# Set-up of a fused spectral-filter and MLP kernel: pools freed tile by tile, and the last inverse unit ahead of the first half's outputs

## The chip, the cores and the metric

The kernel runs on one core of one Trainium2 chip. The metric is the device time of one execution in microseconds, lower is better. Before the change it took 786.47 us (median of three runs, 786.09 to 787.12). All runs in this document were in the fast state: no run was more than 1.5% above the fastest of its kernel. Verdicts are given at 2%, with a 95% interval for the ratio of two kernels. The whole effect studied here is under 0.5%, so every verdict reads "same", and what decides is the stretches within the traces.

The engines go by the profile's names: PE (TensorE, the matmuls), ACT (ScalarE), DVE (VectorE), POOL (GpSimd) and SP (SyncE, which issues transfers). A result of PE lands in a bank of PSUM; "to evacuate" it means that ACT or DVE copies it from there to SBUF.

## The reference

```python
# x: 8 x 3008 x 256, filters 1505 x 256, w_in 256 x 2048, w_out 2048 x 256, all float32
X = np.fft.rfft(x, axis=1)
Y = X * (filt_r + 1j * filt_i)[None]
y = np.fft.irfft(Y, n=3008, axis=1)            # 8 x 3008 x 256
t = y.reshape(24064, 256)
h = t @ w_in                                   # 24064 x 2048
g = h * (1.0 / (1.0 + np.exp(-beta * h)))
out = (g @ w_out).astype(np.float32)           # 24064 x 256
```

## The kernel before

The transform of length 3008 = 47 x 64 is done as four stages of small matmuls with tables (`t1`, `t2`, `t3` and its rotated copy `t3s`, `t4`). The first batch goes through SBUF as fast as it can, because nothing else can run until its output `y` is there. That is the set-up, about the first 43 us. After it comes a loop of 47 blocks of 16 steps: two `hps` matmuls, a Silu on ACT into `gT`, four `acc` matmuls, with the transforms of batches 1 to 7 threaded in by a plan (`at(step, function)`).

In the set-up the inverse half is a chain for each half `e` of the 256 columns: three units `s3_0` (16 matmuls each, evacuated to `zT`), four turns `z_turn` (eight PE transposes each, evacuated to `zz0`), then outputs, either eight small ones `f_0` (4 matmuls, 376 columns to evacuate) or four big ones `s4_0` (8 matmuls, 752 columns). Units 0 to 2 are the first half, 3 to 5 the second. The first half uses `f_0`, the second `s4_0`.

```python
tw = dict(reuse_waits="tile")     # a pool on released memory waits tile by tile, not for all users
spsum = right.enter_context(tc.tile_pool(name="spsum", bufs=3, space=bass.MemoryType.PSUM))  # 3 x 2 banks
tpsum = right.enter_context(tc.tile_pool(name="tpsum", bufs=2, space=bass.MemoryType.PSUM))  # 2 x 1 bank
units = [(0, 0), (1, 0), (2, 0), (0, 1), (1, 1), (2, 1)]     # (group of tables, half e)

def evac(dst, src, on_act, scale=None):
    if on_act:
        nc.scalar.activation(dst, src, ACT.Copy, scale=1.0 if scale is None else scale)
    elif scale is None:
        nc.vector.tensor_copy(dst, src)
    else:
        nc.vector.tensor_scalar_mul(dst, src, scale)

def bank2(shape, dt=F32):
    return spsum.tile(shape, dt, name="sps", tag="sps")
def turn8():
    return tpsum.tile([P, KH, P], BF16, name="tps", tag="tps")

def z_turn(e, hh, on_act, wide=False):            # transposes of zT -> zz0
    tp = bank2([P, KH, P], BF16) if wide else turn8()
    ...
def s3_0(n, engines=(True,)):                     # pq_t x tables -> zT
    one = len(engines) == 1
    tiles = [bank2([P, KH, P])]
    tiles.append(tiles[0] if one else bank2([P, KH, P]))   # two engines: two PSUM tiles
    ...
def f_0(e, u, on_act):                            # 4 output groups, a tpsum tile
def s4_0(e, hh, on_act):                          # 8 output groups, an spsum tile
# ...
s3_0(3)
s2_0(5)
f_0(0, 0, True); f_0(0, 1, True)
z_turn(0, 2, True); z_turn(0, 3, True)
s3_0(4)
f_0(0, 2, True); f_0(0, 3, True); f_0(0, 4, False)
s3_0(5, (False, True))
f_0(0, 5, True); f_0(0, 6, False); f_0(0, 7, True)
z_turn(1, 0, False); z_turn(1, 1, True); z_turn(1, 2, False, True); z_turn(1, 3, True, True)
s4_0(1, 0, False); s4_0(1, 1, True); s4_0(1, 2, False); s4_0(1, 3, True)
```

(The order of the tail is put several calls to a line here.) A `True` in a call means that ACT evacuates, `False` that DVE does. The fourth argument of `z_turn` takes a wide PSUM buffer. Which of the three wide or two small buffers a tile gets is decided when the program is built. It isn't a strict rotation, and the source doesn't show it.

Of the kernel before, what the change touches and what calls it, by code (L numbers as in the profile page):

```python
# [36 lines left out]
def kernel(  # L37
# [30 lines left out]
        )  # L68
    )

    dpool = ctx.enter_context(tc.tile_pool(name="dram_scratch", bufs=2, space=bass.MemoryType.DRAM))
    consts = ctx.enter_context(tc.tile_pool(name="consts", bufs=1))
    wpool = ctx.enter_context(tc.tile_pool(name="wpool", bufs=1))

    xpool = ctx.enter_context(tc.tile_pool(name="xpool", bufs=4))
    apool = ctx.enter_context(tc.tile_pool(name="apool", bufs=4))
    ypools = [ctx.enter_context(tc.tile_pool(name="ypool0", bufs=1))]
    fr_sb = consts.tile([P, NK, D], F32, name="fr_sb", tag="fr_sb")
    fi_sb = consts.tile([P, NK, D], F32, name="fi_sb", tag="fi_sb")
# [29 lines left out]
# [7 lines that stand above are left out]
# [3 lines left out]
    def rpool(name, stack=right, **kw):  # L119
        return stack.enter_context(tc.tile_pool(name=name, side="right", **kw))  # L120

    tw = dict(reuse_waits="tile")
    spsum = right.enter_context(
        tc.tile_pool(name="spsum", bufs=3, space=bass.MemoryType.PSUM)
    )
    tpsum = right.enter_context(
        tc.tile_pool(name="tpsum", bufs=2, space=bass.MemoryType.PSUM)
    )
    sp = rpool("setup", bufs=1)

# [5 lines that stand above are left out]
# [216 lines left out]
        nc.sync.dma_start(rows[:, g * JG : (g + 1) * JG, :], st["a1", b][:])  # L352

    left = ExitStack()
    wst = ctx.enter_context(tc.tile_pool(name="wstage", bufs=2))
    zpool0 = left.enter_context(tc.tile_pool(name="zpool0", bufs=1))
    WG = 4
    wstage = {}
# [33 lines left out]
    def z_turn(e, hh, on_act, wide=False):  # L392
        tp = bank2([P, KH, P], BF16) if wide else turn8()
        for i in range(KH):
            j0 = (hh * KH + i) * KP
            nc.tensor.transpose(tp[:, i, :], zT[e][:, j0 : j0 + P], ident[:])  # L396
        evac(zz0[:, hh * KH : (hh + 1) * KH, e * P : (e + 1) * P], tp[:KP], on_act)

    def s4_0(e, hh, on_act):
        ps = bank2([P, JG, P])  # L400
        for i in range(JG):
            nc.tensor.matmul(
                ps[:, i, :NP],
                lhsT=zz0[:, hh * JG + i, e * P : (e + 1) * P],
                rhs=t4[:],
                start=True,
                stop=True,
            )
        dst = ys[0][:, e, :].rearrange("p (n j) -> p n j", j=J)
        evac(  # L410
            dst[:, :, hh * JG : (hh + 1) * JG],
            ps[:, :, :NP].rearrange("p j n -> p n j"),
            on_act,
            inv_scale,
        )

    pq = {}
    r_p0 = ExitStack()
    p0pool = rpool("p0pool", r_p0, bufs=2)

    def s2_0(n):
        kg, e = units[n]
        ds = slice(e * P, (e + 1) * P)
        ks = slice(kg * KH, (kg + 1) * KH)
        ps = bank2([P, KH, P])
        for kk_ in range(KH):
            k1 = kg * KH + kk_
            nc.tensor.matmul(
                ps[:, kk_, :], lhsT=t2[:, k1, :], rhs=a0[:, k1, ds], start=True, stop=True
            )  # L430
        for c, filt in enumerate((fr_sb, fi_sb)):
            r_t = p0pool.tile([P, KH, P], BF16, name="pq_t", tag=f"pq{c}")
            nc.vector.tensor_tensor(r_t[:], ps[:], filt[:, ks, ds], ALU.mult)
            pq[n, c] = r_t

    def s3_0(n, engines=(True,)):
        kg, e = units[n]
        one = len(engines) == 1
        tiles = [bank2([P, KH, P])]
        tiles.append(tiles[0] if one else bank2([P, KH, P]))  # L440
        for c, tab in enumerate((t3, t3s)):
            src = pq.pop((n, c))
            for kk_ in range(KH):
                nc.tensor.matmul(  # L444
                    tiles[kk_ // 4][:, kk_, :],
                    lhsT=src[:, kk_, :],
                    rhs=tab[:, kg * KH + kk_, :],
                    start=c == 0 and kk_ % 4 == 0,
                    stop=c == 1,
                    skip_group_check=True,  # L450
                )
        kq = P // J
        dst = zT[e][:, :WZ].rearrange("p (j k) -> p j k", k=KP)
        for h, on_act in enumerate(engines):
            n0, n1 = (0, KH) if one else (4 * h, 4 * h + 4)
            k0 = kg * KH
            evac(
                dst[:, :, (k0 + n0) * kq : (k0 + n1) * kq],
                tiles[h][:, n0:n1, :].rearrange("p k (c j) -> p j (k c)", j=J),
                on_act,  # L460
            )
# [9 lines left out]
    def f_0(e, u, on_act):  # L471
        ps = tpsum.tile([P, 4, P], F32, name="tps", tag="tps")
        for i in range(4):
            nc.tensor.matmul(
                ps[:, i, :NP],
                lhsT=zz0[:, 4 * u + i, e * P : (e + 1) * P],
                rhs=t4[:],
                start=True,
                stop=True,
            )  # L480
        dst = ys[0][:, e, :].rearrange("p (n j) -> p n j", j=J)
        evac(
            dst[:, :, 4 * u : 4 * u + 4],
            ps[:, :, :NP].rearrange("p j n -> p n j"),
            on_act,
            inv_scale,
        )
# [40 lines left out]
    s3_0(3)  # L528
    s2_0(5)
    f_0(0, 0, True)  # L530
    f_0(0, 1, True)
    z_turn(0, 2, True)
    z_turn(0, 3, True)
    s3_0(4)
    f_0(0, 2, True)
    f_0(0, 3, True)
    f_0(0, 4, False)
    s3_0(5, (False, True))
    f_0(0, 5, True)
    f_0(0, 6, False)  # L540
    f_0(0, 7, True)
    z_turn(1, 0, False)
    z_turn(1, 1, True)
    z_turn(1, 2, False, True)
    z_turn(1, 3, True, True)
    s4_0(1, 0, False)
    s4_0(1, 1, True)
    s4_0(1, 2, False)
    s4_0(1, 3, True)
    r_p0.close()  # L550
    r_sr.close()
    right.close()
# [242 lines left out]
```

## Time and profile before

| quantity, before | value |
|---|---|
| time, median of 3 | 786.47 us |
| span of the profiled run | 785.6 us |
| first `hps` matmul of the loop | 42.71 us |
| PE idle in the loop (waits from 42.7 us on) | 2.3 us in three waits |
| stall of PE on the first scratch load (`a<-d`) | 1.2 us |

The windows view gives busy time by stretch. Its columns are the stretch and its length, then busy us and instructions of PE, PE's weight loads, DVE, ACT and POOL, the granted TensorE clock, the mean busy share of the DMA engines as the tool adds it up (it can pass 1), and GB/s. These lines are of before.

```profile
30.00:40.00 10.00, 6.97 (x124) 6.42 (x121) 5.28 (x7) 7.63 (x13) 5.59 (x6) 1.00 1.06 214
...
50.00:60.00 10.00, 10.00 (x69) 6.65 (x68) 1.37 (x2) 8.21 (x14) 4.78 (x4) 1.00 0.78 216
...
200.00:785.00 585.00, 580.75 (x4487) 412.54 (x4485) 306.84 (x479) 412.67 (x601) 84.42 (x77) 1.00 0.36 100
```

There are two regimes. In the loop PE hardly rests (580.75 of 585 us), so it only moves as a block. In the set-up no engine is full: PE 6.97 and ACT 7.63 of 10 us between 30 and 40 us. There each engine waits for another, and only the chain of dependencies counts. A change of the set-up is worth the time by which it lets the block start earlier.

The timeline of PE in before, from the first turns on (start, duration, engine, source line, operation, tiles, count, and in brackets the idle time before it and what ended it). L444 is `s3_0`, L396 `z_turn`, L474 `f_0`, L726 and L746 the loop.

```profile
26.55 0.62 PE L396 MATMUL tps<-ident,zT 128*128 128x128 bf16 x8 [0.22 <-ACT zT L111]
28.28 0.61 PE L396 MATMUL tps<-ident,zT 128*128 128x128 bf16 x8 [1.11 <-ACT zz L111]
...
33.91 0.33 PE L474 MATMUL tps<-t,zz 96*128 96x94 bf16 x4 [0.51 <-ACT zz L111]
35.19 0.33 PE L474 MATMUL tps<-t,zz 96*128 96x94 bf16 x4 [0.96 <-ACT y L111]
35.36 0.61 PE L444 MATMUL sps<-t,pq_t 128*128 128x128 bf16 x8
...
42.71 0.59 PE L726 MATMUL hps<-y,win_sb 128*128 128x512 bf16 x2 [0.89 <-ACT y L111]
...
45.38 0.60 PE L746 MATMUL acc<-wout_sb,gT 128*128 128x256 bf16 x4
```

The line at 35.36 is what the change aims at: the last inverse unit, `s3_0(5)`, starts behind small outputs that waited 0.51 and 0.96 us for small PSUM buffers. Everything of the second half hangs on that unit. The line at 28.28: two turns in a row were given the same small bank, and the second one waited 1.11 us for the evacuation of the first.

Two clocks are used from here on. **S** is the stretch from the start of the first turn to the start of the first `acc` group: 45.38 - 26.55 = 18.83 us in before. The **body** is from that `acc` group to the end of the span, 785.6 - 45.38 = 740.2 us.

The list of PE's waits in the loop of before (from 42.7 us on; total us, times, longest) has two entries. The first is a load from scratch memory in the loop, at about 62.6 us.

```profile
PE ps L588 <- DMA a<-d: 1.2, 1, 1.2
PE hps L726 <- ACT y L111: 1.1, 2, 0.9
```

### The profile page before, as it was taken

To read this page: it belongs to the slowest core of one execution; us is meant where nothing else is said; L and a number is where in the kernel's file an instruction comes from. 1 tells how busy PE (TensorE), PEld (TensorE's weight loads), DVE (VectorE), ACT (ScalarE), POOL (GpSimd) and SP (SyncE) were. 2 spreads that over 40 slices of the span, in tenths; PEclk is the share of its full clock that TensorE was granted. 3 is DMA by queue.
4 is the path that set the end of the run, shared out by engine and by line. 5 is a ranking of instruction groups with operands and counts; after the bars stand their busy time and mean duration, and the time that the engine had idled before them with its cause. 6 is when DMAs were issued, how large, how long until landed. Compare 5 with 4: busy or idle time off the path is not lost.

```text
span 785.6 us, 15256 instructions
## 1 busy us (share of the span) xinstructions
PE 768.7 (98%) x6071; PEld 544.7 (69%) x6071; DVE 437.1 (56%) x679; ACT 560.8 (71%) x826; POOL 151.9 (19%) x160
## 2 busy tenths in 40 slices
PE   8699999999999999999999999999999999999997
PEld 5666767766677666866678666786667767676664
DVE  7746754777557665566655665466655666321001
ACT  6787867767676766777667776677766777777775
POOL 6723400332012220122201222012200222000000
PEclk9999999999999999999999999999999999999999
DMA  9968286233831349123580426612164111500101
GB/s 175 228 175 196 79 223 169 68 88 96 240 95 51 95 126 256 39 76 107 115 241 29 120 62 156 199 57 86 48 188 121 61 48 49 155 28 28 55 28 55
DMA packets 89819, 88.51 MB, mean 113 GB/s; under 512 B 5692, under 2 KB 80956, under 8 KB 89748
## 3 DMA queue, kind: packets, MB, share of 16 engines
q1 hardware_dynamic: 85716, 73.94, 32.1%
q0 software_dynamic: 4032, 13.60, 10.3%
q8 instruction: 47, 0.77, 0.4%
q14 instruction: 24, 0.20, 0.1%
HBM read 54.47 MB, written 46.66 MB: 129 GB/s over the span
## 4 chain that ended last, share of the span: by engine, by line
PE 94%; ACT 3%; DMA 1%; DVE 1%; issue 0%; POOL 0%; POOLq 0%; DVEq 0%; ACTq 0%
PE acc L746 42%; PE hps L726 41%; PE ps L572 3%; PE ps L639 2%; PE ps L588 2%; PE ps L617 2%; DMA a<-d 1%; ACT zz L111 1%; ACT zT L111 1%; ACT y L111 0%; ACT aT L111 0%; PE tps L396 0%; ACT t3s L291 0%; PE sps L444 0%; ACT a L111 0%
## 5 line engine op out<-in xcount | busy, mean ns | idle before, releaser
L735 ACT ACTIVATE gT<-hps,beta_sb 128x512 bf16<-128x512 f32 x752 | 516.9, 687 | 208.8 <-PE hps L726 206.2
L746 PE MATMUL acc<-wout_sb,gT 128*128 128x256 bf16 x3008 | 453.4, 272 | 0.0
L726 PE MATMUL hps<-y,win_sb 128*128 128x512 bf16 (+7 forms) x1728 | 448.0, 351 | 1.1 <-ACT y L111 1.1
L746 PEld LDWEIGHTS <-gT 128*128 128x128 bf16 x3008 | 287.5, 98 | 126.2 <-issue 1.2
L607 POOL TENSOR_TENSOR yh<-a_t,b_t 128x512 bf16<-128x512 f32 x84 | 106.4, 1267 | 421.8 <-DVE b_t L606 420.9
L726 PEld LDWEIGHTS <-win_sb 128*128 128x128 bf16 x1728 | 164.9, 98 | 25.2 <-issue 1.2
L113 DVE COPY ost<-acc 128x512 f32<-128x512 f32 x93 | 59.9, 686 | 147.6 <-PE acc L746 147.6
L113 DVE CAST a<-ps 96x512 bf16<-96x512 f32 x104 | 70.8, 685 | 52.5 <-PE ps L572 48.4
L602 DVE TENSOR_TENSOR a_t<-ps,fr_sb 128x512 f32<-128x512 f32 x84 | 58.1, 692 | 71.3 <-PE ps L588 70.8
L115 DVE TENSOR_SCALAR y<-ps 128x376 bf16<-128x376 f32 x104 | 56.0, 548 | 59.3 <-PE ps L639 59.1
L603 DVE SCALAR_TENSOR_TENSOR b_t<-ps,fi_sb 64x512 f32<-64x512 f32 x84 | 58.2, 692 | 1.1
L606 DVE TENSOR_TENSOR b_t<-ps,fi_sb 64x512 f32<-64x512 f32 x84 | 57.4, 683 | 1.1
L113 DVE CAST z<-ps 128x512 bf16<-128x512 f32 x72 | 49.3, 684 | 1.7 <-PE ps L617 0.8
L639 PEld LDWEIGHTS <-zz 96*128 96x128 bf16 x448 | 29.8, 98 | 22.9
L572 PE MATMUL ps<-xg,t 94*96 94x512 bf16 x112 | 41.5, 381 | 0.0
L639 PE MATMUL ps<-t,zz 96*128 96x94 bf16 x448 | 34.7, 205 | 0.0
L588 PE MATMUL ps<-a,t 128*128 128x256 bf16 x168 | 32.1, 273 | 1.2 <-DMA a<-d 1.2
L617 PE MATMUL ps<-yh,t 128*128 128x256 bf16 x168 | 32.1, 273 | 0.0
L617 PEld LDWEIGHTS <-t 128*128 128x128 bf16 x168 | 16.2, 98 | 17.7
L588 PEld LDWEIGHTS <-t 128*128 128x128 bf16 x168 | 16.1, 98 | 16.6 <-issue 1.5
L171 POOL DMA_DIRECT2D xg<-in_x_dram x24 | 12.4, 519 | 56.5 <-PE ps L572 56.5
L572 PEld LDWEIGHTS <-t 94*96 94x96 bf16 x112 | 13.8, 123 | 10.5
(104 smaller groups left out, 184.3 us busy)
## 6 DMA issues: line engine op xcount, KB each, us to landing
out_dram<-ost SPq DMA_DIRECT2D x46, 512.0 KB, 3.0
d<-a SPq DMA_DIRECT2D x28, 384.0 KB, 4.5
a<-d SPq DMA_DIRECT2D x28, 384.0 KB, 5.2
d<-z SPq DMA_DIRECT2D x28, 384.0 KB, 3.7
zz<-d SPq DMA_DIRECT2D x28, 384.0 KB, 6.5
xg<-in_x_dram POOLq DMA_DIRECT2D x24, 384.0 KB, 6.5
ws<-in_moe_w_out_dram SPq DMA_DIRECT2D x4, 512.0 KB, 5.9
fr_sb<-in_filt_r_dram SPq DMA_DIRECT2D x12, 128.0 KB, 4.9
```

The source lines that it names most:

```text
L113: nc.vector.tensor_copy(dst, src)
L572: nc.tensor.matmul(ps[:KP], lhsT=t1[:], rhs=xg[b, g][:NP, jj : jj + 2, :], start=True, stop=True)
L588: nc.tensor.matmul(ps[:, e, :], lhsT=t2[:, k0 + e, :], rhs=st["a2", b, g][:, kk + e, :], start=True, stop=True,)
L602: nc.vector.tensor_tensor(a_t[:], ps[:], fr_sb[:, ks, :], ALU.mult)
L603: nc.vector.scalar_tensor_tensor(b_t[:M], ps[M:], -1.0, fi_sb[M:, ks, :], ALU.mult, ALU.mult)
L606: nc.vector.tensor_tensor(b_t[M:], ps[:M], fi_sb[M:, ks, :], ALU.mult)
L607: nc.gpsimd.tensor_tensor(yh[:], a_t[:], b_t[:], ALU.add)
L617: nc.tensor.matmul(ps[:, e, :], lhsT=t3[:, 2 * i + e, :], rhs=yh[:, e, :], start=True, stop=True)
L639: nc.tensor.matmul(ps[:, e, :NP], lhsT=zz[:, j0 % JG + e, dc * P : (dc + 1) * P], rhs=t4[:], start=True, stop=True,)
L726: nc.tensor.matmul(hps[:, pos - t0 : pos - t0 + ln], lhsT=win_sb[:, dc, fb * P : (fb + 1) * P], rhs=ys[b][:, dc, n0 : n0 + ln], start=(dc ...
L735: nc.scalar.activation(gT[:], hps[:], ACT.Silu, scale=beta_sb[:, fb : fb + 1])
L746: nc.tensor.matmul(acc[tb // 2][:, tb % 2, :], lhsT=gT[:, tb * P : (tb + 1) * P], rhs=wout_sb[:, fb, :], start=(fb == 0 and tb % 2 == 0), ...
```

## The change

The intent has two parts. The pools of the set-up get `reuse_waits="tile"`, so that a pool that lands on released memory waits only for the tile in its place. And the last unit `s3_0(5)` and the second half's turns go ahead of most outputs of the first half: those outputs need no more input and can fill gaps, while the second half is the longer chain. Two evacuations go from ACT to DVE on balance.

```diff
+    tw = dict(reuse_waits="tile")
-    xpool = ctx.enter_context(tc.tile_pool(name="xpool", bufs=4))
+    xpool = ctx.enter_context(tc.tile_pool(name="xpool", bufs=4, **tw))
 # ... the same for apool, spsum, tpsum, wstage and p0pool
@@ the order of the tail
     s3_0(3)
     s2_0(5)
     f_0(0, 0, True)
+    z_turn(0, 2, True)
     f_0(0, 1, True)
-    z_turn(0, 2, True)
     z_turn(0, 3, True)
     s3_0(4)
-    f_0(0, 2, True)
+    s3_0(5, (False, True))
+    z_turn(1, 0, False, True)
+    z_turn(1, 1, True, True)
+    f_0(0, 2, False)
+    z_turn(1, 2, False, True)
+    z_turn(1, 3, False, True)
     f_0(0, 3, True)
+    s4_0(1, 0, True)
     f_0(0, 4, False)
-    s3_0(5, (False, True))
     f_0(0, 5, True)
-    f_0(0, 6, False)
-    f_0(0, 7, True)
-    z_turn(1, 0, False)
-    z_turn(1, 1, True)
-    z_turn(1, 2, False, True)
-    z_turn(1, 3, True, True)
-    s4_0(1, 0, False)
-    s4_0(1, 1, True)
-    s4_0(1, 2, False)
-    s4_0(1, 3, True)
+    s4_0(1, 1, False)
+    f_0(0, 6, True)
+    s4_0(1, 2, True)
+    f_0(0, 7, False)
+    s4_0(1, 3, False)
```

## The prediction

> **What bounds the kernel now.** The window table of before shows two regimes. From 42.7 us to the end PE is busy 10.0 of 10 us in nearly every stretch, and the PE wait list after 42.7 us has two entries, together 2.3 us (the last set-up output, and one load of `a<-d`, 1.2 us, at 62.6). That part moves only as a block. The set-up before it is bound by dependencies: PE 7 to 9 busy of 10 us, ACT 7.5 to 8.7. In the chain of waits 26 to 42.7 us alternates between ACT evacuations and short PE groups. The first `hps` matmul starts at 42.71, 0.05 us after the last `y` evacuation of ACT. So the change is worth what it takes off 42.71.
>
> **What it removes, adds, moves.** No matmul or evacuation is added or removed.
>
> (a) Pool waits by tile. `xpool`, `apool`, `spsum`, `tpsum` and `wstage` seem to land on nothing that was released; `p0pool` lands on `setup_x`, whose users are done by about 13 us, before its first tile (16.45). The pools that follow were already by tile, and the first `hps` waits for `y` data anyway. I expect 0 us, at most 0.1.
>
> (b) Order. Before, `s3_0(5)` runs at 35.36 behind `f_0(0,2..4)`, which wait for `tps` buffers: PE sat idle 0.51 us (for `zz`) and 0.96 us (for `y`) there. Then come three more outputs of the first half, the turns of the second at 37.6 to 39.5 and four big outputs in a row at the tail. After, `s3_0(5)` follows `s3_0(4)` directly, its turns use the wide pool, and the small outputs fill gaps between turns and big outputs. One turn's evacuation goes from ACT to DVE (1.02 to 0.69 us) and one small output too (0.48 to 0.55).
>
> **Costed by hand.** I walked both orders with durations of the timeline: 8 transposes 0.45 us, `s3_0` 0.89, `f_0` 0.17, `s4_0` 0.35 of PE issue, plus 0.17 to the last result; ACT 1.02, 0.80, 0.60, 0.48; DVE 0.69, 0.94, 0.69, 0.55; 0.05 from one engine to another. The Trainium skill (ScalarE: Activation LUTs, What ACT_TABLE_LOAD costs) gives 186 ns + 0.833 ns an element and an overlap of about 93 ns back to back; the trace agrees (1.02 us for 1024 elements, starts 0.92 apart). The walk of before ends at 42.9 (measured 42.71); of after at 41.3: `s3_0(5)` at about 33.5, turns 35.3 to 37.5, the last `y` evacuation on DVE (`s4_0(1,3)`, behind `f_0(0,7)`), near 41.1. So 1.6 us, nearly all on the critical path.
>
> **Passed on?** `win_sb` landed at 35.7 and the four `xg` loads between 37.4 and 43.4, each still before its need when all needs move by 1.6 us. The `d`, `a2` and `ws` transfers move with the block, so the 1.2 us stall on `a<-d` stays.
>
> **Prediction.** 784.9 us, 8 in 10 between 784.2 and 785.8. Faster by over 2%: 0; within 2%: 0.99; slower: 0.01.
>
> **What shows it.** First `hps` near 41.1; `s3_0(5)` about 1.8 us earlier; PE idle before 41 us about 1.5 us less; the stretch from first `hps` to the end unchanged to 0.2 us.
>
> **What would make it wrong.** A poor choice of PSUM buffers: they aren't strictly rotated (before, two successive turns waited for the same bank, 1.11 us idle), so a wide turn or big output could wait for a slow evacuation and cost 0.5 to 1 us. An `xg` load that lands late. The `a<-d` stall growing. Noise of 0.5 us between runs.

## More of the kernel before

Early in the set-up, DVE makes the rotated table, and POOL copies filter rows to the other partitions:

```python
def t3_rotate(k0, k1, on_act):      # the first call, t3_rotate(1, KH, False), is on DVE: two instructions
    ...
        nc.vector.tensor_scalar_mul(dst, src, rot[c][:])     # t3s <- t3, SBUF to SBUF
def spread(n):
    nc.gpsimd.tensor_copy(fr_sb[M:, ks, ds], fr_sb[:M, ks, ds])
    nc.gpsimd.tensor_copy(fi_sb[:M, ks, ds], fi_sb[M:, ks, ds])
```

And early in the loop, POOL issues the loads of batch 2, and SP the first loads of batch 1 back from scratch memory:

```python
for g in range(NG):
    at(o + 10, a2_load, 1, g)                      # SP: a <- d
# ...
for g in range(4):
    at(o + 14 + 3 * g, load_x, 2, g)               # POOL: xg <- in_x, four loads
```

## The result, and the profile after

After: 786.33 us, median of four runs (787.47, 787.05, 785.5, 785.61). Before had 786.8 us in the four runs compared with it. The ratio is 0.9993, with an interval of 0.9973 to 1.0014. A ratio here comes from the runs of the same rounds and lies within 0.0002 of the ratio of their means, so it is not quite the ratio of the medians. The prediction of 784.9 us, with 785.8 as its upper end, was wrong: hardly any gain is to be seen.

| profiled run | before | after |
|---|---|---|
| span | 785.6 | 785.4 |
| first turn starts | 26.55 | 26.93 |
| S (first turn to first `acc`) | 18.83 | 18.13 |
| body (first `acc` to end of span) | 740.2 | 740.3 |
| time minus span | 1.75 | 2.07 |
| stall on the first `a<-d` | 1.2 | 1.3 |

The set-up did get shorter, by 0.70 us in S, though by less than half of what was predicted. The first turn was 0.38 us later, in a part that the change doesn't touch, and the time outside the span grew by 0.3 us. The timeline of PE in after, the lines that answer to those of before:

```profile
26.93 0.62 PE L396 MATMUL tps<-ident,zT 128*128 128x128 bf16 x8 [0.22 <-ACT zT L112]
...
33.91 0.39 PE L444 MATMUL sps<-t,pq_t 128*128 128x128 bf16 x4
35.20 0.38 PE L444 MATMUL sps<-t,pq_t 128*128 128x128 bf16 x4 [0.90 <-ACT zT L112]
...
41.83 0.38 PE L726 MATMUL hps<-y,win_sb 128*128 128x512 bf16 x1 [0.43 <-ACT y L112]
42.59 0.39 PE L726 MATMUL hps<-y,win_sb 128*128 128x512 bf16 x1 [0.38 <-DVE y L116]
...
45.06 0.60 PE L746 MATMUL acc<-wout_sb,gT 128*128 128x256 bf16 x4
```

`s3_0(5)` starts at 33.91, right behind `s3_0(4)`, but does only four matmuls. Its second PSUM tile waits 0.90 us, until 35.20, for ACT to evacuate the `zT` of `s3_0(4)`. So most of the unit runs hardly earlier than before (35.36). The chain of waits in after says the same (start, duration, what; a chain lists the work that held up the end):

```profile
33.21 1.02 ACT zz L112
34.23 0.92 ACT zT L112
...
35.20 0.84 PE sps L444 x12
...
40.29 2.25 DVE y L116 x3
...
42.59 0.39 PE hps L726
```

The evacuation of `zT` stands in the chain right before the twelve matmuls. Nothing in the arithmetic asks for that: the two units read different inputs. Only a PSUM buffer that both use can make the one wait for the other. The buffers of the built program confirm it: `s3_0(4)` got banks 0 and 1; the two tiles of `s3_0(5)` got banks 4 and 5, and again 0 and 1. Banks 2 and 3 were free: their last reader, a filter multiply on DVE, ended at 33.05. The built program of before gives the same buffers to these two units. There it cost nothing, because ACT had emptied the buffer (at 34.77) before `s3_0(5)` began at 35.36.

The end of the chain is DVE, which evacuates outputs without a break, and whose last one starts at 41.60 and ends at 42.53. The timeline of DVE in after:

```profile
40.29 0.94 DVE L116 TENSOR_SCALAR y<-sps 128x752 bf16<-128x752 f32 x1
41.15 0.54 DVE L116 TENSOR_SCALAR y<-tps 128x376 bf16<-128x376 f32 x1
41.60 0.93 DVE L116 TENSOR_SCALAR y<-sps 128x752 bf16<-128x752 f32 x1
```

And the list of PE's waits in the loop of after still has the stall on the scratch load:

```profile
PE ps L588 <- DMA a<-d: 1.3, 1, 1.3
```

Two theories stand against each other for the missing gain. The first is the PSUM buffer of `s3_0(5)`. Its rival says that DVE, busy without a break at the end, sets the end in any case, so that an earlier `s3_0(5)` would only wait longer. A third thing needs an answer as well: the runs of one kernel differ by up to 2.8 us (before in the third call below, 785.94 to 788.78), more than the effect.

### The profile page after: what moved, and what is told of

It reads as the page before. It is cut to its first block, busy times and chain, and to the rows that moved or that the text cites. A ratio compares the mean times of both kernels' runs of the same rounds, so it can differ in the third digit from the quotient of the medians.

```text
span 785.4 us, 15166 instructions
## 1 busy us (share of the span) xinstructions
PE 764.4 (97%) x5978; PEld 544.5 (69%) x6071; DVE 438.2 (56%) x681; ACT 559.4 (71%) x824; POOL 151.6 (19%) x160
## 4 chain that ended last, share of the span: by engine, by line
PE 93%; ACT 2%; DMA 1%; issue 1%; DVE 0%; ACTq 0%
PE acc L746 43%; PE hps L726 38%; PE ps L572 3%; PE ps L639 3%; PE ps L617 3%; PE ps L588 2%; DMA a<-d 1%; ACT zT L112 1%; ACT zz L112 1%; ACT t3s L291 0%; DVE y L116 0%; PE sps L396 0%; PE sps L444 0%; PE tps L396 0%; ACT a L112 0%
## 5 line engine op out<-in xcount | busy, mean ns | idle before, releaser
L726 PE MATMUL hps<-y,win_sb 128*128 128x512 bf16 (+7 forms) x1636 | 428.3, 350 | 1.1 <-ACT y L112 0.6
```

Of the source, the lines that this page charges most:

```text
L726: nc.tensor.matmul(hps[:, pos - t0 : pos - t0 + ln], lhsT=win_sb[:, dc, fb * P : (fb + 1) * P], rhs=ys[b][:, dc, n0 : n0 + ln], start=(dc ...
```

## The experiments

Fifteen kernels ran, and all of them gave correct results. They are told in four calls; the kernels of a call ran on the same chip (the first two calls on one, the third and the fourth on two others). A table with S of all of them stands at the end of this section.

### First call: the parts of the change, and the bank

**The change again**, unedited, to see how far single profiles and times repeat.

> The changed kernel again, for its runs in the same rounds as its variants. Measure inside the profile: S, from the start of the first turn of zT to the start of the first acc group (before 45.38-26.55=18.83 us; after 45.06-26.93=18.13). Theory A (a wait for a PSUM bank took 0.9 of the 1.6 us): S again 18.1, PE idle 0.9 us inside the third unit of inverse matmuls of the second half, on ACT zT. Rival N (nothing was lost, the first profile was an unlucky one): S scatters by 0.5 us or more. Whole time 0.3 to 1.0 us under before, hidden by 1 us of scatter.

Measured: 786.83 us median (785.55 to 787.39), ratio 1.0001 [0.9988, 1.0013]. S was 18.13 again, to 0.01 us. But there was no stall on `a<-d` in this profile, and the first turn was at 27.59 us, 1.0 us later than in before. So S repeats, while what comes before and after it is subject to something else.

**Only the waits**: the order of before with `**tw` on the six pools.

```diff
 # after, with the order of the tail as in before
     s3_0(4)
-    s3_0(5, (False, True))
-    ...
+    f_0(0, 2, True)
+    f_0(0, 3, True)
+    f_0(0, 4, False)
+    s3_0(5, (False, True))
+    ...
```

> Only the pools' waits, the order of before. All theories but one: PE's program and waits are the same as before, S 18.8, time as before within noise. Rival W (the finer waits cost or gain by themselves): S differs by more than 0.2 us.

Measured: 786.01 us, ratio 0.9996 [0.9983, 1.0008]; S 18.83, as in before. In the built program PE's instructions and waits are those of before; one DVE instruction lost five DMA waits that had long been met. The waits by tile are worth nothing here.

**Only the order**: after without `**tw`.

```diff
-        tc.tile_pool(name="spsum", bufs=3, space=bass.MemoryType.PSUM, **tw)
+        tc.tile_pool(name="spsum", bufs=3, space=bass.MemoryType.PSUM)
 # ... the same for the other five pools
```

> Only the order, the pools' waits of before. Theory A: S 18.1 as after, with the same 0.9 us PE idle on ACT zT. Rival W: S differs from after by more than 0.2 us.

Measured: 785.75 us, ratio 0.9991 [0.9977, 1.0004]; S 18.13. The 0.70 us is all of the order's.

**The bank**: after, with the wide buffers named one by one. The list repeats what the builder chose, except that the second tile of `s3_0(5)` gets the pair that was free, and the later tiles on those two pairs trade places.

```diff
-        tc.tile_pool(name="spsum", bufs=3, space=bass.MemoryType.PSUM, **tw)
+        tc.tile_pool(name="spsum", bufs=1, space=bass.MemoryType.PSUM, **tw)
+    sps_slots = iter([0, 1, 2, 0, 1, ...])            # one entry for each wide tile
     def bank2(shape, dt=F32):
-        return spsum.tile(shape, dt, name="sps", tag="sps")
+        k = next(sps_slots)
+        return spsum.tile(shape, dt, name="sps", tag=f"sps{k}")
```

> The changed kernel, its three wide PSUM buffers named by hand: same sequence up to the fifth inverse unit, but the second half of the sixth unit takes the buffer that is free instead of the one that ACT has just begun to evacuate. Theory A: the 0.9 us idle goes, S 17.2 to 17.4, time about 0.9 us under after. Rival D (DVE, busy without a break over the last 5 us of the set-up, sets the end whatever the bank): the idle goes but S stays near 18.1.

Measured: 785.2 us, ratio 0.9979 [0.9967, 0.9992]; S 17.08. The timeline of PE in this kernel:

```profile
26.31 0.62 PE L399 MATMUL tps<-ident,zT 128*128 128x128 bf16 x8 [0.22 <-ACT zT L112]
...
33.29 0.61 PE L447 MATMUL sps<-t,pq_t 128*128 128x128 bf16 x8
33.73 0.61 PE L447 MATMUL sps<-t3s,pq_t 128*128 128x128 bf16 x8
35.07 1.07 PE L399 MATMUL sps<-ident,zT 128*128 128x128 bf16 x16 [0.72 <-ACT zT L112]
...
43.39 0.60 PE L749 MATMUL acc<-wout_sb,gT 128*128 128x256 bf16 x4
```

The wait of 0.90 us is gone, and `s3_0(5)` starts 6.98 us after the first turn, against 8.81 in before: 1.83 us earlier, as the prediction had said (about 1.8). S is 1.05 us shorter than in after, more than the wait itself, and 1.75 us shorter than in before. That settles the first question: S fell even a little more than forecast (17.2 to 17.4). The rival falls: DVE ends the chain, but it moves up with its inputs, so it doesn't hold the end fast.

### What makes the runs scatter

With the profiles of before, after and the first call side by side, two places differ from run to run while the program is the same.

The first is at 14 us. DVE's two rotations of the table took 1.15 us together in before, 1.36 in after, 0.68 in the waits-only kernel and 2.18 in the repeat of the change. At the same time POOL starts its filter copies, at a moment set by when the filters land from DRAM. In the repeat, the timeline of POOL shows:

```profile
13.86 1.04 POOL L467 COPY fr_sb<-fr_sb 64x1024 f32<-64x1024 f32 x1 [3.44 <-DMA fr_sb<-in_filt_r_dram]
14.96 1.04 POOL L468 COPY fi_sb<-fi_sb 64x1024 f32<-64x1024 f32 x1
```

and that of DVE in the same run:

```profile
13.97 2.18 DVE L293 TENSOR_SCALAR t3s<-t,rot 128x448 bf16<-128x448 bf16 x2
16.07 0.67 DVE L114 COPY a<-sps 128x1024 bf16<-128x1024 bf16 x1
```

Each of the two rotations (1.08 and 1.18 us in the list of that tile) took as long as the POOL copy that had begun before it. The Trainium skill, "SBUF — State Buffer", section "Who interferes with whom", says that copies and `tensor_scalar` on DVE can run in a mode that needs the port pair shared with GpSimd, that the first to issue holds it for a whole instruction, and that the other fully blocks. The trace agrees in size (2.18 us against 0.59 us without overlap, below); which mode DVE ran in it doesn't show. What the trace adds is that a DMA's landing time decides who is first, so the loss differs from run to run.

The second is at 56 us, where POOL issues two loads of `xg` and SP the first loads of `a<-d` almost at once. The timeline of after, with its DMA issues (SPq is SP's queue) and the matmul that waits:

```profile
55.49 1.05 POOL L171 DMA_DIRECT2D xg<-in_x_dram  x2
...
55.82 1.55 SPq L580 DMA_DIRECT2D a<-d  x3
...
63.59 0.38 PE L588 MATMUL ps<-a,t 128*128 128x256 bf16 x2 [1.30 <-DMA a<-d]
```

The DMA view of after for the first of these `a<-d` loads:

```profile
DMA to landing us min/median/max: 7.7/7.7/7.7
```

The same two issues in the timeline of the waits-only kernel, where PE didn't wait:

```profile
55.83 1.05 POOL L171 DMA_DIRECT2D xg<-in_x_dram  x2
...
55.98 0.99 SPq L580 DMA_DIRECT2D a<-d  x2
```

and its DMA view for the first `a<-d` load:

```profile
DMA to landing us min/median/max: 5.9/5.9/5.9
```

If the `a<-d` load follows the first of the `xg` loads by 0.33 us, it lands after 7.7 us and PE stands still; if by 0.15 us, it lands after 5.9 us and PE doesn't. Over all profiles in which the two loads meet, the stall was there at gaps of 0.29, 0.33, 0.41 and 0.49 us, and absent at 0.07 to 0.15 us. The Trainium skill, "DMA: Bandwidth & Descriptors", section "Issuing engines are not separate DMA queues", says that transfers started by different engines run on the same 16 DMA engines and interleave, which is consistent with this: with the `xg` loads moved away, the first `a<-d` landed after 3.2 to 3.5 us.

### Second call: both races taken out

Four kernels got the same two edits. POOL's first filter copy is put behind the rotation by a copy of one element that the rotation writes last, and the `xg` loads are issued eight steps later.

```diff
+    gate = sp.tile([P, 1], BF16, name="gate", tag="gate")
+    nc.gpsimd.tensor_copy(gate[:], t3s[:, KH - 1, P - 1 : P])
     spread(0)
@@
                 for g in range(4):
-                    at(o + 14 + 3 * g, load_x, 2, g)
+                    at(o + 22 + 3 * g, load_x, 2, g)
```

**Before without the races:**

> The order and waits of before, with two timing races taken out: POOL's first filter copy waits for DVE's first table rotation, and the two first x loads for the third batch are issued after 66 us instead of beside the a<-d loads. Theory R (these two races make the 1 to 2 us of scatter between runs): first zT turn at 26.3 us, no PE wait for a<-d, rotation 0.76 us, S 18.83, span 784.0 with all five runs within 0.6 us of each other. Rival (the scatter comes from elsewhere, such as the granted clock): runs still spread over 1.3 us or more.

Measured: 785.93 us (787.26, 785.92, 785.93, 785.96, 785.79), ratio 0.9994 [0.9982, 1.0007]. The five runs spread over 1.47 us, which is the forecast of the rival, not of theory R. But four of them lie within 0.17 us. The fifth is the profiled one, and its trace shows why. The windows view, in the columns explained above (PEclk is third from the end):

```profile
37.00:38.00 1.00, 0.61 (x8) 0.61 (x8) 0.29 (x1) 0.44 (x2) 0.00 (x0) 0.69 1.04 209
38.00:39.00 1.00, 1.00 (x12) 1.00 (x11) 0.25 (x1) 0.38 (x1) 0.00 (x0) 0.50 1.12 229
39.00:40.00 1.00, 1.00 (x12) 1.00 (x10) 0.44 (x1) 0.40 (x1) 0.00 (x0) 0.50 1.06 209
40.00:41.00 1.00, 1.00 (x14) 1.00 (x13) 0.54 (x1) 0.62 (x1) 0.00 (x0) 0.61 1.02 205
```

The granted clock fell to 0.50. From the four means, the time at half clock is estimated at (1 - 0.69) / 0.5 + 1 + 1 + (1 - 0.61) / 0.5 = 3.4 us. Asked for the stretch from 37.40 to 40.80, the same view gives 0.50, and 1.00 for the 3.4 us on either side of it. S became 20.12 instead of 18.83. The Trainium skill, "TensorE: Matmul & The Clock Gate", section "What's actually happening", gives two clocks, half and full, and a free-running window of about 3.4 us; the trace agrees with the two clocks and with the length, in this one dip. The same page, "Part 4: PE-mode transpose", says that transposes don't count as busy in the same way. The dip lies in the stretch with the 32 transposes of the second half, but before's profile has the same stretch at full clock (1.00 between 38 and 39 us). The dip also began at 37.4, ahead of the first of these transposes (37.66), and ended, at 40.8, about when they did. In the 3.4 us before it PE was busy for only 1.72 us, and for 1.79 us in the same stretch of before, which kept its clock. And the clock came back after 3.4 us of nearly nothing but transposes, so in this dip they did not keep it down. It was seen in one profile of seventeen, so the cause is not shown here.

**After without the races:**

> The changed kernel with the same two races taken out. Theory A+R: S 18.13, so 0.7 us under x1_before_norace in every pair, and this now shows in the times (span 783.3). Rival N: no difference in time beyond 0.3 us.

Measured: 785.54 us, and all five runs between 785.54 and 785.57; ratio 0.9986 [0.9974, 0.9999]; S 18.13. The timeline of POOL in this kernel shows the gate doing its work:

```profile
14.79 0.19 POOL L490 COPY gate<-t3s 128x1 bf16<-128x1 bf16 x1 [4.20 <-DVE t3s L293]
15.04 1.03 POOL L467 COPY fr_sb<-fr_sb 64x1024 f32<-64x1024 f32 x1
```

and DVE's rotation takes 0.59 us, ahead of it:

```profile
14.13 0.59 DVE L293 TENSOR_SCALAR t3s<-t,rot 128x448 bf16<-128x448 bf16 x2
```

With a scatter of 0.03 us the change can be read from times at last: 785.93 - 785.54 = 0.39 us by the medians. That is less than the 0.7 us that was expected to show, although S is 0.70 us shorter. The third and fourth calls look for the other 0.3 us.

**The bank without the races**: the list of wide buffers and both edits.

> x2_after_norace with the wide PSUM buffers named by hand, so that the sixth inverse unit takes the free one. Theory A: S 17.08, 1.05 us under x2_after_norace (span 782.3), so the whole 1.6 to 1.8 us against x1_before_norace that was predicted for the change.

Measured: 784.54 us (784.34 to 784.91), ratio 0.9974 [0.9962, 0.9987]; S 17.08, the same as with the races.

**A second bank**: the small buffers named as well, so that the second turn takes the other bank than the first (the 1.11 us at 28.28 of before).

```diff
+    tps_slots = iter([0, 1, 1, 0, 1, 0, ...])
     def turn8():
-        return tpsum.tile([P, KH, P], BF16, name="tps", tag="tps")
+        return tpsum.tile([P, KH, P], BF16, name="tps", tag=f"tps{next(tps_slots)}")
```

> x3_bank_norace with the two small PSUM buffers named by hand too: the second turn of the first half takes the buffer other than the first turn's, which waited 1.11 us for ACT. By the walk of the order the turn then waits for DVE's copy only, 0.66 us less: S 16.4, span 781.6. Rival D (ACT is the limit in that stretch, the wait only moves): S stays at 17.0.

Measured: 783.84 us (783.68 to 784.04), ratio 0.9964 [0.9951, 0.9978]; S 16.40. The second turn now waits 0.42 us, in the timeline of PE:

```profile
27.54 0.61 PE L400 MATMUL tps<-ident,zT 128*128 128x128 bf16 x8 [0.42 <-DVE a L114]
```

That is 0.69 us less, and S is 0.68 us shorter. The kernel before its change has the same wait of 1.11 us; what S would gain there was not tested.

In all six kernels with the gate (two of them come in the later calls) the rotation takes 0.59 or 0.60 us and the first turn starts between 26.47 and 26.49 us, so the first race is out. Not all scatter is, though: the five runs of the bank kernel and of the second-bank kernel without races still spread over 0.57 and 0.36 us. Where that comes from is not known.

### Third call: the time outside the span

The difference of time and span was 1.73 to 1.82 us in every run so far of the kernels with before's order, and 2.03 to 2.15 in every run of those with after's. A guess was that the length of some engine's program decides it, and PE's was tried first: one start-up matmul more or fewer.

```diff
 # on before
-    spin(15)
+    spin(16)
 # on after
-    spin(15)
+    spin(14)
```

> Before with one more idle matmul at the start (two more PE instructions, 12156 as the changed kernel has, instead of 12154). In all runs so far the time is 1.73 to 1.82 us over the span with the old order and 2.04 to 2.15 with the new one. Theory P (the number of PE instructions sets this part): 2.0 to 2.15 us. Rival Q (the evacuations' new split over ACT and DVE, or anything else in the order): 1.73 to 1.82 as before.

> The changed kernel with one idle matmul less at the start (12154 PE instructions). Theory P: 1.73 to 1.82 us over the span. Rival Q: 2.04 to 2.15 as the changed kernel has.

Measured: before with 16 took 786.58 us, ratio 1.0 [0.9984, 1.0017], time minus span 1.73 to 1.80. After with 14 took 786.56 us, ratio 0.9993 [0.9977, 1.001], time minus span 2.05 to 2.12. Neither moved: the guess was wrong.

**The tail**: the second-bank kernel with three outputs on other engines, so that DVE has one small output less at the end.

```diff
     f_0(0, 6, True)
-    s4_0(1, 2, True)
-    f_0(0, 7, False)
-    s4_0(1, 3, False)
+    s4_0(1, 2, False)
+    f_0(0, 7, True)
+    s4_0(1, 3, True)
```

> x4_bank2_norace with the last small output and the last big output on ACT and the third big output on DVE. By the walk of the order, DVE's unbroken run at the end gets one output shorter: S 16.15 to 16.3 instead of 16.40, span 781.4 to 781.6. Rival: the last output still starts when its matmuls do, S 16.4.

Measured: 783.49 us (783.48 to 783.51), ratio 0.9956 [0.9943, 0.9968]; S 16.25, only 0.15 us under 16.40. So the unbroken run of DVE at the end, which looked like the limit, was worth 0.15 us. Time minus span was 1.88 to 1.91, which fits neither group. That gave the next guess: this kernel has one ACT instruction more than the one that it came from.

**Only the loads moved**: after with the `xg` loads eight steps later, without the gate.

```diff
-                    at(o + 14 + 3 * g, load_x, 2, g)
+                    at(o + 22 + 3 * g, load_x, 2, g)
```

> The changed kernel with only the two x loads moved away from the a<-d loads; the rotation still races with POOL's copies. Theory R: no PE wait for a<-d in the profile, and the five spans spread only by the first race, 783.2 to 784.7 us. Rival: a span of 785 us or more still comes up.

Measured: 785.56 us (785.38 to 786.24), ratio 0.9983 [0.9971, 0.9996]. The spans were 783.3, 783.5, 783.4, 784.2 and 783.6, where the change alone had spans of 783.4 to 785.4. The stall was out of the profile, and what scatter is left is of the size of the first race.

### Fourth call: ACT's instruction count

Three kernels add tiny ACT copies in the loop, far from the critical path.

```diff
+    dum = consts.tile([P, 2], BF16, name="dum", tag="dum")
+    for k in range(2):          # 1 in the other two kernels
+        at(400 + 8 * k, nc.scalar.activation, dum[:, k : k + 1], ident[:, :1], ACT.Copy)
```

After with two of them (as many ACT instructions as before has), after with one, and the tail kernel with one:

> The changed kernel with two more ACT instructions (copies of one column, in the body where ACT has slack), so ACT has 1595 as before has. Time over span so far: 1.72 to 1.82 us at 1595 ACT instructions, 1.88 to 1.91 at 1594 (y3_tail), 2.03 to 2.16 at 1593. Theory L (the length of ACT's program sets this part): 1.7 to 1.85 us. Rival O (something else of the order): 2.03 to 2.16 still.

> The changed kernel with one more ACT instruction, 1594. Theory L: 1.85 to 1.95 us over the span. Rival O: 2.03 to 2.16.

> y3_tail with one more ACT instruction, 1595. Theory L: 1.7 to 1.85 us over the span, so 783.35 us in place of 783.49. Rival O: 1.88 to 1.91 as y3_tail.

Measured: after with two took 786.12 us, ratio 0.9989 [0.9972, 1.0005], time minus span 1.73 to 1.82. After with one took 786.39 us, ratio 0.9993 [0.9977, 1.0009], time minus span 1.93 to 1.96. The tail kernel with one took 783.3 us (783.11 to 783.32), ratio 0.9952 [0.9934, 0.9970], time minus span 1.79 to 1.82.

The page of each profile counts the instructions of the engines. The line of before:

```profile
PE 768.7 (98%) x6071; PEld 544.7 (69%) x6071; DVE 437.1 (56%) x679; ACT 560.8 (71%) x826; POOL 151.9 (19%) x160
```

that of after (some matmul records are missing from this trace, so PE's count is not to be read here):

```profile
PE 764.4 (97%) x5978; PEld 544.5 (69%) x6071; DVE 438.2 (56%) x681; ACT 559.4 (71%) x824; POOL 151.6 (19%) x160
```

and that of after with one ACT copy:

```profile
PE 769.2 (98%) x6071; PEld 544.4 (69%) x6071; DVE 438.4 (56%) x681; ACT 560.0 (71%) x825; POOL 151.7 (19%) x160
```

In all kernels together: 826 ACT instructions on the page go with 1.72 to 1.82 us outside the span, 825 with 1.88 to 1.96, 824 with 2.03 to 2.16. DVE's count doesn't order them: at 681 all three groups occur. The copies leave the order and the instruction counts of the other engines as they were, so ACT's count is shown to move this part, for the three counts tried: an instruction more on ACT makes the time outside the span shorter. (In the tail kernel the whole time went from 783.49 to 783.30 us too, but on different chips.) Why is left open; the trace shows nothing outside the span, and no run here tests lengths other than these three.

### All of them

| kernel | S | time minus span | median us | ratio to before of the same rounds |
|---|---|---|---|---|
| before | 18.83 | 1.72 to 1.82 | 786.47 | |
| after | 18.13 | 2.05 to 2.11 | 786.33 | 0.9993 |
| the change again | 18.13 | 2.05 to 2.13 | 786.83 | 1.0001 |
| only the waits | 18.83 | 1.74 to 1.82 | 786.01 | 0.9996 |
| only the order | 18.13 | 2.04 to 2.13 | 785.75 | 0.9991 |
| the bank | 17.08 | 2.03 to 2.13 | 785.20 | 0.9979 |
| before without the races | 20.12 in the profile with the clock dip | 1.73 to 1.82 | 785.93 | 0.9994 |
| after without the races | 18.13 | 2.04 to 2.07 | 785.54 | 0.9986 |
| bank without the races | 17.08 | 2.04 to 2.14 | 784.54 | 0.9974 |
| both banks without the races | 16.40 | 2.04 to 2.15 | 783.84 | 0.9964 |
| before, one PE matmul more | 18.82 | 1.73 to 1.80 | 786.58 | 1.0000 |
| after, one PE matmul fewer | 18.12 | 2.05 to 2.12 | 786.56 | 0.9993 |
| tail | 16.25 | 1.88 to 1.91 | 783.49 | 0.9956 |
| after, loads moved | 18.13 | 2.04 to 2.16 | 785.56 | 0.9983 |
| after, two ACT copies | 18.13 | 1.73 to 1.82 | 786.12 | 0.9989 |
| after, one ACT copy | 18.13 | 1.93 to 1.96 | 786.39 | 0.9993 |
| tail, one ACT copy | 16.24 | 1.79 to 1.82 | 783.30 | 0.9952 |

The sum can be checked on the kernels without races, by medians against before without the races (785.93), whose S without the dip is taken as 18.83. After: S -0.70, outside +0.30, so -0.40; measured -0.39. The bank: -1.75 + 0.30 = -1.45; measured -1.39. Both banks: -2.43 + 0.30 = -2.13; measured -2.09. Two terms account for these medians to within 0.06 us.

The last line of the table beats both kernels: 783.3 us against 786.32 for before in the same rounds.

## Why the prediction was wrong

- **What bounds the kernel: right.** The body was 740.2 us in before and 740.3 in after, and 738.8 to 739.1 in all profiles without the `a<-d` stall. It moves as a block.
- **The waits by tile, "I expect 0 us, at most 0.1": right.** The waits alone left S at 18.83, the order alone gave 18.13.
- **The order, "`s3_0(5)` follows `s3_0(4)` directly ... at about 33.5": this is the step that failed.** The walk let `s3_0(5)` run through its 0.89 us of PE issue once PE and its inputs were ready, and took free PSUM buffers for granted. It did start there (33.91, of which 0.38 us is the later first turn), but only with four matmuls. A buffer was free, but the builder gave the second tile the one of `s3_0(4)`, which ACT had still to evacuate: PE sat idle 0.90 us, and the other twelve matmuls started at 35.20. PE's idle time from the first turn to 41 us fell by 0.68 us (4.44 to 3.76), not by about 1.5. With the free buffer named by hand, `s3_0(5)` came 1.83 us earlier against the first turn (predicted about 1.8), and S fell by 1.75 us (predicted 1.6). The mechanism was right, and the missing term measured 1.05 us. The prediction named this risk, on the strength of the 1.11 us at 28.28, and sized it at 0.5 to 1 us. But it kept it out of its sum: 784.9 plus 0.5 to 1 is 785.4 to 785.9, which its range, up to 785.8, covered without the 0.3 us below.
- **The time outside the span was not in the sum.** The two evacuations that went from ACT to DVE cost 0.3 us there. The profile of before shows nothing of it, because the span leaves it out.
- **Together**: 1.75 - 1.05 - 0.30 = 0.40 us of gain, where 1.6 was predicted. Before had 786.8 us in the runs compared with after, and 786.8 - 0.4 = 786.4, close to the 786.33 measured. With four runs of each that spread over 2 us, so close a match is luck. The race-free pair, 0.39 us, is what carries the sum.
- **The last evacuation, `s4_0(1,3)` on DVE: right in kind, 1.4 us late** (ended at 42.53, predicted 41.1). First `hps` matmuls ran at 41.83 and 42.59 instead of 41.1. Of this, 0.38 us is the later first turn, and the bank's 1.05 us is the rest. That DVE is the limit there was tempting and small: moving outputs off it gave 0.15 us.
- **"The 1.2 us stall on `a<-d` stays": not a fixed cost.** It is a race of two issues within half a microsecond. It was in four of the seventeen profiles, absent from six in which the same two loads met, and from all seven in which the `xg` loads were moved. The loads of `win_sb` and `xg` never held PE up, as predicted.
- **"Noise of 0.5 us between runs": too small.** The runs of before spread from 785.94 to 788.78 us. Two races are shown with their sizes, 0.1 to 1.6 us of extra DVE time at 14 us and 1.2 to 1.3 us of PE at 62 us, and one dip of the clock added 1.3 us to S. Without the two races, five runs of after agree to 0.03 us, but those of two other kernels only to 0.36 and 0.57 us. Which of them struck in a given run that wasn't traced is not known.

## What to carry to other kernels

When an order is walked by hand, walk the PSUM buffers too: look up which bank the built program gave each tile, because a tile that gets a bank still being read turns an independent step into a dependent one, here 1.05 of 1.75 us. Where the effect is smaller than the scatter, find the races that make the scatter (two starts that a DMA's landing puts in either order) and take them out of both kernels; then 0.4 us could be read from the medians here. Compare a fixed stretch of the program in the traces, such as S here, which repeated to 0.01 us while times moved by 2 us, except in the one profile with the clock dip.

## What the Trainium skill lacked or had wrong

Nothing that the runs touched was found plainly wrong; one remark, on transposes and the clock, sits badly with the one dip seen. The other points were missing.

- "PSUM — Partial Sum Buffer": it has no word on what it costs when the program builder gives a tile a bank that is still being read while another is free. Here it was 0.90 us of PE idle time and 1.05 us of S for one tile, and 0.68 us of S for another.
- "DMA: Bandwidth & Descriptors": it says that transfers of different engines interleave on the same 16 DMA engines, but not how much the order of two nearly simultaneous issues matters. Here the first 384 KB load landed after 7.4 to 7.7 us when issued 0.29 to 0.49 us behind the first of two loads of the other queue, after 5.5 to 5.9 us when 0.07 to 0.15 us behind, and after 3.2 to 3.5 us without them.
- "SBUF — State Buffer": the blocking is there and agrees, but not that it makes runs differ when a DMA's landing releases one of the two. Here DVE's pair of rotations took 0.59 to 2.18 us, and the first turn started at 26.3 to 27.6 us.
- "TensorE: Matmul & The Clock Gate": the two clocks and the window agree (0.50 for 3.4 us). It doesn't say how often PE loses the clock in the middle of a busy kernel: here in one of seventeen profiles, at a cost of 1.3 us, and with no cause shown. Its remark that transposes don't count as busy in the same way would not lead one to expect that full clock came back after 3.4 us of nearly nothing but transposes, as it did there.
- No page has this: the time outside the span went with ACT's instruction count, 1.72 to 1.82 us at 826 instructions on the page, 1.88 to 1.96 at 825, and 2.03 to 2.16 at 824. Its cause is open.
